# Attention and ELU layer on one core: the probabilities of four groups are turned by VectorE and a round trip through DRAM

## The chip, the core and the metric

One core of a Trainium2 chip runs the whole program. The metric is the device time of one execution in microseconds (us). The kernel before took 598.57 us, the median of 3 runs (598.29 to 599.19). A measurement of this kernel can tell about 0.2% (1.2 us) from no change.

## The reference

Four batches, eight heads, 576 positions, 64 features per head. Each head is causal softmax attention plus a read of a memory matrix; both are mixed by a gate, and the result goes through a two-layer network with ELU. All in float32.

```python
scores = np.where(causal, -1e9, q @ k.T / 8)
a = np.exp(scores - scores.max(-1)); a /= a.sum(-1)
local = a @ v
q_p = phi(q)
mem_out = (q_p @ M_prev) / (q_p @ z_prev)
x = g * mem_out + (1 - g) * local
h = x @ w_in
out = np.where(h > 0, h, np.exp(h) - 1) @ w_out
```

`x` has 2304 rows of 512, `w_in` is 512 x 2048 and `w_out` 2048 x 512.

## The kernel before

The 2304 rows are cut into nine groups of 256. Group 0 holds the first 64 positions of all four batches. Groups 1 to 4 hold positions 64 to 319 of one batch each (`hf` = 0), and groups 5 to 8 hold positions 320 to 575 (`hf` = 1, up to 576 keys). Attention runs by groups in that order, and within a group by four pairs of heads. The network runs in 144 chunks, 16 for each group; a chunk is 128 of the 2048 hidden features. Three groups are split in two parts, so that the network can start while weights still arrive.

Attention of one head in groups 5 to 8, for each of two blocks of 128 queries (`j`):

- scores on TensorE (`add_split`, L787), the product of a key tile with a high and a low part of the query;
- the mask and the row maximum on VectorE (`add_red`, L801), into a row `pt` of 128 queries by 512 or 640 columns, of which the first 64 hold the memory query (`add_mem`, L545);
- the exponential on ScalarE (L832), the reciprocal of the sum on VectorE (L553, L556), and the scaling of the probabilities on ScalarE, VectorE or GpSimd (L848, L850, L852);
- `add_blocks`: each 128 x 128 block of the row is transposed by TensorE against an identity matrix (L878) into a PSUM tile `t`, and copied, nearly always by ScalarE, into `pth` in SBUF (L884). The first block of queries has 4 blocks in one copy, the second has 5 in two copies (3 and 2);
- `pv` in `add_pair` (L739): the turned rows are multiplied with the memory matrix and the values. From group 3 on, one step takes four heads (two pairs) at once, 40 matmuls in groups 5 to 8. It needs the `pth` of all four.

A chunk of the network (`add_ff`) is 12 matmuls of 256 columns (L901), an ELU on ScalarE and VectorE (L916, L919, L922, L931, L934), and 6 matmuls of 512 columns (L965).

The order of all work is made when the program is built. `Plan` holds operations with a priority, the engines that may do each and what each takes by formulas (`dve`, `act`, `dma`, ...), and `Plan.order` plays them through: the operation that can start first goes next, and the priority settles ties. The result is one fixed order of instructions per engine; on the chip an engine waits at an instruction that isn't ready, even if a later one is. All DMAs are issued by SyncE (SP), in that same order. `UBEG`, `UDUE` and `P_ADD` set the priorities of attention by group, `W_ADD` those of the weights. A DMA is taken to land `DMA_LAT` = 2600 ns after its own cost.

A `Ring` is a set of buffers given out in order (`RB` has their numbers). `p` has 2 buffers (one pair of heads), `pth` 4 (two pairs), `kq` 1, `st` 2 (raw weights, and output rows), `wf` 2 (weights in work), `ev` 3 (parts of sums on their way to DRAM).

Of the kernel before, what the change touches and what calls it, by code (L numbers as in the profile page):

```python
# [22 lines left out]
HALF_NK = (320, 576)  # L23
HALF_QCS = ((1, 2), (3, 4))
HALF_NCH = (3, 5)
HALF_RUNS = (((0, 0, 192), (1, 0, 320)),), (((0, 0, 448), (1, 0, 64)), ((1, 64, 576),))
PITCH = 512
SIGN = -0x80000000
REBIAS = 2.0 ** -112
MASKED = -8e9  # L30
# [9 lines left out]
SN = 2  # L40
TN = 2
SPLIT = (4, 7, 11)
UDUE = (-29, 4, 17, 55, 62, 81, 65, 101, 114)
UBEG = (-44, -1, 11, 22, -4, 67, 91, 58, 99)
RB = {'mn': 10, 'rs': 4, 'p': 2, 'pth': 4, 'v': 4, 'ks': 1, 'qh': 1, 'ql': 1, 'kq': 1, 'ev': 3}
BIAS = {'POOL': -400, 'DVE': -150, 'DV2': -250, 'ACT': -750}
E_OFF = 162
FIRST_ACT = 4
# [2 lines left out]
RELU_PHI = 0  # L51
PHI_MIN = -1
W_LATE = (1, 0, -4, -14)
W_ADD = (0, 6, -1, 0, -1, -2, -8, 3, 1, -3, -3, -1, 5, 11, -8, 0, 4, -5, 1, 8, 16, -16, -5, 2, -10, 1, 2, 7, -10, -18, 1, 1)
P_ADD = (-19, -2, 17, 2, -1, 0, -1, 1, 0, -1, 0, 0, 0, -1, -1, -2, -10, 18, -15, -1, 0, 0, 1, -17, 0, -10, 7, -7, 10, -2, 8, 9, 5, 10, 0, -1)
W_OFF = 4
SLACK = 0
WARM_BEG = 1100.0
# [244 lines left out]
def kernel(  # L303
# [22 lines left out]
        kw = {"space": bass.MemoryType.PSUM} if psum else {}  # L326
        return Ring(ctx.enter_context(tc.tile_pool(name=name, bufs=bufs, **kw)), name, bufs, shape, dtype)

    kq_r = ring("kq", RB.get("kq", 2), [128, 832])
    v_r = ring("v", RB.get("v", 2), [128, 6, 64])  # L330
    qz_r = ring("qz", RB.get("qz", 2), [128, 8, 64])
    ks_r = ring("ks", RB.get("ks", 1), [128, S], F32R)
# [4 lines left out]
    p_r = ring("p", RB.get("p", 2), [128, 1152])  # L337
    mn_r = ring("mn", RB.get("mn", 8), [128, 4])
    rs_r = ring("rs", RB.get("rs", 3), [128, 4])
    pth_r = ring("pth", RB.get("pth", 3), [128, 1152])  # L340
    ev_r = ring("ev", RB.get("ev", 2), [128, G])
    xh_r = ring("xh", RB.get("xh", 3), [128, 4, G], F32R)
    xl_r = ring("xl", RB.get("xl", 3), [128, 4, G], F32R)
# [316 lines left out]
    def add_pair(u, pair, qp, rn):  # L660
        b, hf = units[u]
        nk, nch, q0h = HALF_NK[hf], HALF_NCH[hf], HALF_Q0[hf]
        h0 = 2 * pair
        p0 = unit_prio(u, (h0 - 0.5) / NH)
        vs = []
        if hf == 0:
            v = v_r.new()

            def ld_v():
                nc.sync.dma_start(  # L670
                    out=v.t.rearrange("p (h c) d -> p h c d", h=2), in_=vx[b, h0:h0 + 2, :, 0:3].rearrange("h p c d -> p h c d")
                )
# [12 lines left out]

        pts, pths, rs = [p_r.new() for _ in range(2)], [pth_r.new() for _ in range(2)], rs_r.new()
        for i in range(2):
            add_mem(p0, qp, rn, pts[i], 2 * i, 2, PITCH)
        mns = {}
        runs = (HALF_RUNS if NATIVE[u] else RUN_SPLIT)[hf]  # L690
        if NATIVE[u]:
            kqt = kq_r.new()
            if hf == 0:
                add(p0 - 4, [("SP", dma(0.5 * (nk + G)), lambda: nc.sync.dma_start(out=kqt.t[:, 0:nk + G], in_=kqp[b, pair]))], w=[kqt])
            else:
                for i in range(2):
                    def ld(i=i):
                        nc.sync.dma_start(out=kqt.t[64 * i:64 * i + 64, 0:nk + G], in_=kq1[b, h0 + i, 0:64])

                    add(p0 - 4, [("SP", dma(0.25 * (nk + G)), ld)], w=[(kqt, i)])  # L700
            for n, run in enumerate(runs):
                add_scores(u, h0, n / len(runs), run, kqt, nk, pts, mns)
        else:
            for i in range(2):
                kqt = kq_r.new()

                def ld(kqt=kqt, i=i):
                    nc.sync.dma_start(out=kqt.t[:, 0:nk + G], in_=(kq0, kq1)[hf][b, h0 + i])

                add(p0 - 4 + i, [("SP", dma(0.5 * (nk + G)), ld)], w=[kqt])  # L710
                split = split_head(u, h0 + i, kqt)
                for n, run in enumerate(runs):
# [12 lines left out]
        for c in range(nch):
            lo = max(0, (128 * c - 64) - q0h) if c else 0
            mm.append((c, lo, c * G + (0 if c == 4 else lo)))
        late.append([(*vs[i], pths[i]) for i in range(2)])
        if PV_TWO[u] and len(late) < 2:
            return  # L730
        ps = t_r.new()
        todo = late[:]
        late.clear()

        def pv():
            for n, heads in enumerate(todo):
                for i, (c, lo, o) in enumerate(mm):
                    for j, (vj, v0, tj) in enumerate(heads):
                        nc.tensor.matmul(  # L739
                            ps.t[64 * j:64 * j + 64, G * n + lo:G * n + G], vj.t[:, v0 + c], tj.t[:, o:o + G - lo],  # L740
                            start=(i == 0), stop=(i == len(mm) - 1),
                        )

        pp = unit_prio(u, (h0 + 2) / NH)
        cost = TURN_V + len(todo) * sum(pe4(G - lo) for c, lo, o in mm)
        add(pp, [("PE", cost, pv)], r=[x for heads in todo for vj, _, tj in heads for x in (vj, tj)], w=[ps])
        for n in range(len(todo)):
            add_x(u, pp, ps, pair - len(todo) + 1 + n, G * n)
# [3 lines left out]
    def split_head(u, h, kqt):  # L752
# [2 lines left out]
        p0 = unit_prio(u, (h - 0.5) / NH)  # L755
        ks, qh, ql = ks_r.new(), qh_r.new(), ql_r.new()

        def k_hi(eng):
            return lambda: eng(ks.t[:, 0:nk], kqt.t[:, 0:nk])

        def k_lo(eng):
            return lambda: eng.tensor_tensor(
                ks.t[64:128, 0:nk], kqt.t[64:128, 0:nk], ks.t[64:128, 0:nk].bitcast(F32), op=ALU.subtract
            )

        def q_hi(eng):
            return lambda: eng(qh.t, kqt.t[:, nk:nk + G])

        def q_lo(eng):
            return lambda: eng.tensor_tensor(ql.t, kqt.t[:, nk:nk + G], qh.t.bitcast(F32), op=ALU.subtract)  # L770

        add(p0, [("DV2", dve2(nk), k_hi(nc.vector.tensor_copy)), ("ACT", act(nk), k_hi(nc.scalar.copy))], r=[kqt], w=[ks])
        add(p0, [("POOL", pool2(nk), k_lo(nc.gpsimd)), ("DV2", dve(nk), k_lo(nc.vector))], r=[kqt], w=[ks])
# [62 lines left out]
    def add_probs(u, h, j, pt, rs, col, pk, pth):  # L836
# [24 lines left out]
        nblk = qc + 1
        for a, e in ([(0, nblk)] if nblk <= 4 else [(0, 3), (3, nblk)]):
            add_blocks(u, p0, hf, j, a, e, pt, po, pk, pth)

    def add_blocks(u, p0, hf, j, a, e, pt, po, pk, pth):
        ps = t_r.new()
        n = (e - a) * 128
        q0 = 128 * j

        def dst():  # L870
            if a:
                return pth.t[:, a * G + q0:].rearrange("p (c q) -> p c q", q=128)
            m = min(HALF_NCH[hf], 4)
            return pth.t[:, 0:m * G].rearrange("p (c q) -> p c q", q=G)[:, a:e, q0:q0 + 128]

        def tr():
            for c in range(a, e):
                nc.tensor.matmul(  # L878
                    ps.t[:, 128 * (c - a):128 * (c - a) + 128], pt.t[:, po + 128 * c:po + 128 * c + 128], ident,
                    start=True, stop=True, is_transpose=True,  # L880
                )

        def copy(eng):
            return lambda: eng(dst(), ps.t[:, 0:n].rearrange("p (c q) -> p c q", q=128))  # L884

        add(p0, [("PE", 109 * (e - a), tr)], r=pk + [(pt, "m")], w=[ps])
        add(p0, [("ACT", act(n, False), copy(nc.scalar.copy)), ("DVE", dve(n), copy(nc.vector.tensor_copy))], r=[ps], w=[(pth, (j, a))])


    part = nc.dram_tensor('part', (3 * G, DM), F32, kind='Internal').ap()  # L890
    acc_of = {}

    def add_ff(g, c, c0, c1, v):
# [85 lines left out]
        if c1 < NFC:  # L979
# [1 line left out]
                for i in range(2):  # L981
                    add_part(g, t, i, acc[t], pe_)
            return
        osb = st_r.new()

        def view(t):
            return osb.t[:, 512 * t:512 * t + 512].bitcast(F32)

        def fetch(t):
            return lambda: nc.sync.dma_start(out=view(t), in_=part[128 * (2 * g + t):128 * (2 * g + t) + 128])  # L990
# [14 lines left out]

        for t in range(2):
            if c0:
                add(v - 3, [("SP", 800, fetch(t))], r=[f"part{g}{t}"], w=[(osb, t)])
            e_ = "DVE" if c0 or t else "ACT"
            add(pe_, [(e_, (act(512, False) if e_ == "ACT" else dve(512)), ev(t))], r=[acc[t]], w=[(osb, t)])  # L1010
            add(pe_, [("SP", 800, st(t))], r=[(osb, t)])

    def add_part(g, t, i, acc, p):

# [126 lines left out]
```

## Time and profile before

| | before |
|---|---|
| median of 3 runs | 598.57 us (598.29 to 599.19) |
| profiled execution, span from first to last instruction | 597.6 us |
| profiled execution, own time | not listed apart from the span |
| TensorE (PE) busy | 586.7 us, 98% |
| VectorE (DVE) busy | 442.0 us, 74% |
| ScalarE (ACT) busy | 381.1 us, 64% |
| GpSimd (POOL) busy | 73.0 us, 12% |
| DMA moved | 63.85 MB in 32,813 packets |

The span begins with the program's first instruction and ends with its last. Busy time is the time in which at least one instruction of the engine runs. TensorE's matmuls overlap one another, so the sum of their durations exceeds their busy time, and what one costs is read from the distance between starts.

### The profile page before, as it was taken

Reading aid. Unit: us, or ns where it says so; the run is one execution under the profiler, and the core shown is the slowest. Engines: PE = TensorE matmul, PEld = TensorE weight load, DVE = VectorE, ACT = ScalarE, POOL = GpSimd, SP = SyncE. Lnnn points to the kernel's source line nnn. Section 1 sums busy time; section 2 is a strip of 40 time slices with the busy share of each in tenths; the row PEclk is TensorE's granted clock in tenths of the full one; section 3 lists DMA queues with packets and bytes.
Section 4 is the critical chain, followed back from the end, with each engine's and each line's share of the span. In section 5 each row is a group of like instructions: output and inputs, shape, how many; then the busy total and the mean of one; then the engine's idle time right before and its main releaser. Section 6 shows DMA issues by size and latency. Waiting matters only on the chain.

```text
span 597.6 us, 11969 instructions
## 1 busy us (share of the span) xinstructions
PE 586.7 (98%) x4150; PEld 507.0 (85%) x4150; DVE 442.0 (74%) x1394; ACT 381.1 (64%) x1021; POOL 73.0 (12%) x108
## 2 busy tenths in 40 slices
PE   8999999999999999999999999999999999999997
PEld 6766868898898898999888999898889888899996
DVE  6999999999987884477774478687968786444443
ACT  5699889676677872377682377686767776533222
POOL 3333123120011120000120000101111010000000
PEclk9999999999999999999999999999999999999999
DMA  8755756445463332012422022424232323000000
GB/s 264 234 189 183 220 158 209 160 163 185 144 184 113 96 127 72 1 59 90 137 74 59 1 94 74 117 72 154 73 118 74 103 92 103 1 2 28 10 1 36
DMA packets 32813, 63.85 MB, mean 107 GB/s; under 512 B 3568, under 2 KB 17392, under 8 KB 32752
## 3 DMA queue, kind: packets, MB, share of 16 engines
q1 hardware_dynamic: 32752, 63.08, 33.5%
q8 instruction: 33, 0.54, 0.4%
q14 instruction: 28, 0.23, 0.1%
HBM read 56.77 MB, written 6.29 MB: 106 GB/s over the span
## 4 chain that ended last, share of the span: by engine, by line
PE 83%; DVE 12%; ACT 2%; issue 1%; DMA 1%; POOL 0%; DVEq 0%; ACTq 0%; POOLq 0%; SPq 0%
PE acc L965 31%; PE h L901 31%; PE t L739 7%; PE t L878 7%; PE s L787 6%; DVE p L801 2%; DVE st L403 1%; PE acc L1033 1%; DVE wf L406 1%; ACT p L848 1%; DMA p<-in_kqf 1%; DVE gl L934 1%; DVE e L919 1%; DVE p L545 1%; DVE qp L470 1%
## 5 line engine op out<-in xcount | busy, mean ns | idle before, releaser
L901 PE MATMUL h<-xh,w1h 128*128 128x256 f32 x576 | 149.4, 284 | 0.5 <-DVE e L922 0.5
L901 PE MATMUL h<-xl,w1h 128*128 128x256 f32 x576 | 148.1, 281 | 0.0
L901 PEld LDWEIGHTS h<-xh,w1h 128*128 128x128 f32 x576 | 108.4, 188 | 11.9 <-DVE e L922 1.0
L901 PEld LDWEIGHTS h<-xl,w1h 128*128 128x128 f32 x576 | 108.9, 189 | 9.6
L916 ACT ACTIVATE e<-h 128x256 f32<-128x256 f32 x144 | 55.1, 383 | 64.7 <-PE h L901 64.0
L931 ACT CAST gh<-e 128x256 fp32r<-128x256 f32 x143 | 57.8, 404 | 59.2 <-DVE e L922 56.4
L965 PE MATMUL acc<-w2h,gl 128*128 128x512 f32 x288 | 93.5, 403 | 0.0
L965 PE MATMUL acc<-w2h,gh 128*128 128x512 f32 x288 | 92.4, 402 | 0.4 <-ACT gh L931 0.4
L965 PE MATMUL acc<-w2l,gh 128*128 128x512 f32 x288 | 92.8, 402 | 0.0
L901 PEld LDWEIGHTS h<-xh,w1l 128*128 128x128 f32 x576 | 85.0, 189 | 9.2 <-issue 0.5
L901 PE MATMUL h<-xh,w1l 128*128 128x256 f32 x576 | 92.7, 283 | 0.0
L832 ACT ACTIVATE p<-p,mn 128x192 f32<-128x192 f32 (+3 forms) x128 | 78.6, 616 | 18.1 <-DVE mn L801 17.9
L919 DVE TENSOR_SCALAR e<-e 128x256 f32<-128x256 f32 x144 | 43.7, 303 | 51.8 <-ACT e L916 50.4
L934 DVE TENSOR_TENSOR gl<-e,gh 128x256 fp32r<-128x256 f32 x131 | 57.3, 438 | 31.7 <-ACT gh L931 30.9
L884 ACT COPY pth<-t 128x384 f32<-128x384 f32 (+2 forms) x155 | 67.2, 455 | 11.5 <-PE t L878 10.4
L878 PE MATMUL t<-ident,p 128*128 128x128 f32 x448 | 69.3, 274 | 1.2 <-POOL p L852 0.6
L801 DVE CUSTOM_DVE_ANT_0 p<-s,mask 128x192 f32<-128x192 f32 (+3 forms) x128 | 57.9, 476 | 14.8 <-PE s L787 9.7
L878 PEld LDWEIGHTS t<-ident,p 128*128 128x128 f32 x448 | 53.5, 140 | 12.4 <-ACT p L848 2.2
L922 DVE SCALAR_TENSOR_TENSOR e<-h,e 128x256 f32<-128x256 f32 x144 | 60.6, 421 | 2.2
L739 PE MATMUL t<-pth,v 128*64 128x256 f32 (+1 forms) x512 | 54.5, 357 | 1.7 <-ACT pth L884 1.7
L739 PEld LDWEIGHTS t<-pth,v 128*64 128x64 f32 x512 | 34.9, 137 | 20.8 <-ACT pth L884 3.4
L848 ACT ACTIVATE p<-p,rs 128x320 f32<-128x320 f32 (+3 forms) x88 | 47.1, 584 | 6.6 <-DVE rs L556 5.2
(97 smaller groups left out, 818.6 us busy)
## 6 DMA issues: line engine op xcount, KB each, us to landing
kq<-in_kq SPq DMA_DIRECT2D x32, 416.0 KB, 3.1
st<-in_w_in SPq DMA_DIRECT2D x16, 512.0 KB, 3.4
st<-in_w_out SPq DMA_DIRECT2D x16, 512.0 KB, 3.6
qz<-in_qzx SPq DMA_DIRECT2D x32, 224.0 KB, 2.9
v<-in_vx SPq DMA_DIRECT2D x32, 160.0 KB, 2.4
out<-st SPq DMA_DIRECT2D x16, 256.0 KB, 2.1
kq<-in_kqp SPq DMA_DIRECT2D x12, 288.0 KB, 3.3
v<-in_vx SPq DMA_DIRECT2D x16, 192.0 KB, 3.4
```

The costliest lines, as they stand in the source:

```text
L739: nc.tensor.matmul(ps.t[64 * j:64 * j + 64, G * n + lo:G * n + G], vj.t[:, v0 + c], tj.t[:, o:o + G - lo], start=(i == 0), stop=(i == len( ...
L801: nc.vector.tensor_tensor_reduce(out=pts[i].t[:, po + 64 + a:po + 64 + e], in0=ps.t[:, o:o + e - a], in1=m, op0=ALU.add, op1=ALU.min, scal ...
L832: nc.scalar.activation(out=x, in_=x, func=AF.Exp, bias=mn.t[:, 0:1], scale=-1.0, accum_out=rs.t[:, col:col + 1])
L848: eng.activation(out=x, in_=x, func=AF.Copy, scale=c)
L878: nc.tensor.matmul(ps.t[:, 128 * (c - a):128 * (c - a) + 128], pt.t[:, po + 128 * c:po + 128 * c + 128], ident, start=True, stop=True, is_ ...
L884: return lambda: eng(dst(), ps.t[:, 0:n].rearrange("p (c q) -> p c q", q=128))
L901: nc.tensor.matmul(ps.t[:, 0:G], w[:, c, k], x.t[:, k], start=(k == 0 and w is w1h and x is xh), stop=(k == 3 and lo))
L916: nc.scalar.activation(out=at(ee), in_=ps.t[:, 0:G], func=AF.Exp)
L922: nc.vector.scalar_tensor_tensor(at(gg), ps.t[:, 0:G], 0.0, e.t, ALU.max, ALU.add)
L931: return lambda: eng(gh.t, at(gg))
L934: return lambda: eng.tensor_tensor(gl.t, at(gg), gh.t.bitcast(F32), op=ALU.subtract)
L965: nc.tensor.matmul(acc[t].t, a.t[:, 128 * t:128 * t + 128], w[:, c], start=(c == c0 and i == 0), stop=(c == c1 - 1 and i == 2))
```

## The change

In groups 5 to 8 the blocks are no longer transposed by TensorE. For each head and each block of queries VectorE transposes the row in 32 x 32 blocks into `pth`, with the four 32-column strips of the queries side by side (`STEP` = 160 columns each). That leaves the keys spread over the four quadrants of partitions in the wrong order; so each quadrant (32 partitions, 1280 columns) is written to a DRAM buffer `turned` by a DMA of its own, in runs of 160 elements, and one DMA reads the whole 128 x 1280 tile back into the same `pth`. GpSimd clears the columns that the shorter row doesn't fill. `pv` reads its moving operand in runs of 32 elements. Groups 1 to 4 keep the TensorE transposes; the branch for two copies goes away, since at most four blocks are left there.

To make room, `pth` grows to 1280 columns, `kq` shrinks to 576; the keys and queries of groups 5 to 8 are loaded into the `st` ring (2 buffers); output rows go through `wf`; `ev` has 2 buffers. The order constants are new. The branch of `NATIVE` groups with `hf` = 1, which was never taken, is dropped.

```diff
+STEP = 160
-UDUE = (-29, 4, 17, 55, 62, 81, 65, 101, 114)
-UBEG = (-44, -1, 11, 22, -4, 67, 91, 58, 99)
-RB = {'mn': 10, 'rs': 4, 'p': 2, 'pth': 4, 'v': 4, 'ks': 1, 'qh': 1, 'ql': 1, 'kq': 1, 'ev': 3}
+UDUE = (-29, 4, 19, 53, 54, 49, -1, 69, 100)
+UBEG = (-44, -1, 11, 22, 14, 43, 35, 52, 67)
+RB = {'mn': 10, 'rs': 4, 'p': 2, 'pth': 4, 'v': 4, 'ks': 1, 'qh': 1, 'ql': 1, 'kq': 1, 'ev': 2}
...
+def dvt(n):
+    return 145 + 1.1 * n
...
-    kq_r = ring("kq", RB.get("kq", 2), [128, 832])
+    kq_r = ring("kq", RB.get("kq", 2), [128, 576])
-    pth_r = ring("pth", RB.get("pth", 3), [128, 1152])
+    pth_r = ring("pth", RB.get("pth", 3), [128, 8 * STEP])
...
             add_mem(p0, qp, rn, pts[i], 2 * i, 2, PITCH)
+            if hf:
+                add_pad(p0, pths[i])
...
-                kqt = kq_r.new()
+                kqt = (kq_r, st_r)[hf].new()
...
                 add_probs(u, h0 + i, j, pts[i], rs, 2 * i + j, pk[i][j], pths[i])
+            if hf:
+                add_turn(u, h0 + i, pths[i])
...
+                        if hf:
+                            x = tj.t.rearrange("p (s x) -> p s x", x=STEP)[:, lo // 32:8, 32 * c:32 * c + 32]
+                            y = y.rearrange("p (s x) -> p s x", x=32)
...
+        n = (qc + 1) * 128
+        if hf:
+            def turn():
+                x = pt.t[:, po:po + n].rearrange("p (m a i) -> p a m i", a=4, i=32)
+                y = pth.t[:, 4 * STEP * j:4 * STEP * j + 4 * STEP].rearrange("p (a k) -> p a k", k=STEP)[:, :, 0:n // 4]
+                nc.vector.transpose(y.rearrange("p a (m i) -> p a m i", i=32), x)
+
+            add(p0, [("DVE", dvt(n), turn)], r=pk + [(pt, "m")], w=[(pth, j)])
+            return
...
+    def add_pad(p, pth):
+
+        def f():
+            nc.gpsimd.memset(pth.t[:, 0:4 * STEP].rearrange("p (a k) -> p a k", k=STEP)[:, :, 128:STEP], 0.0)
+
+        add(p, [("POOL", 250, f)], w=[(pth, "pad")])
+
+    def add_turn(u, h, pth):
+
+        n = (u - 1 - NB) * NH + h
+        p0 = unit_prio(u, (h + 0.5) / NH)
+        place = turned[128 * n:128 * n + 128]
+
+        def put(c):
+            def f():
+                nc.sync.dma_start(
+                    out=place.rearrange("(a i) (t c x) -> i t a c x", i=32, t=2, c=4)[:, :, :, c],
+                    in_=pth.t[32 * c:32 * c + 32].rearrange("i (t a x) -> i t a x", t=2, a=4),
+                )
+            return f
+
+        for c in range(4):
+            add(p0, [("SP", dma(160), put(c))], r=[pth], w=[(f"turned{n}", c)])
+        add(p0, [("SP", dma(640), lambda: nc.sync.dma_start(out=pth.t, in_=place))], r=[f"turned{n}"], w=[pth])
+
+    turned = nc.dram_tensor('turned', (NB * NH * 128, 8 * STEP), F32, kind='Internal').ap()
...
-        osb = st_r.new()
+        osb = [wf_r.new() for t in range(2)]
```

`W_ADD` and `P_ADD` are new number by number; those of `W_ADD` now go from -58 to 25 (before from -18 to 16), those of `P_ADD` for groups 5 to 8 from -35 to 46 (before from -17 to 10).

## Rows read from the trace of the kernel before

**Rows 1.** The page: busy time by engine, and 40 slices for PE and its clock.

```profile
PE 586.7 (98%) x4150; PEld 507.0 (85%) x4150; DVE 442.0 (74%) x1394; ACT 381.1 (64%) x1021; POOL 73.0 (12%) x108
PE   8999999999999999999999999999999999999997
PEclk9999999999999999999999999999999999999999
```

**Rows 2.** Busy time by stretch: PE, PEld, DVE, ACT, POOL, clock, DMA share, GB/s.

```profile
0.00:30.00 30.00, 26.92 (x299) 21.36 (x300) 23.47 (x110) 18.35 (x66) 9.53 (x18) 1.00 0.77 249
30.00:90.00 60.00, 56.96 (x389) 41.83 (x387) 59.17 (x197) 53.14 (x162) 15.62 (x24) 1.00 0.59 189
205.00:523.00 318.00, 317.70 (x2244) 280.50 (x2240) 225.70 (x705) 203.19 (x511) 28.88 (x43) 1.00 0.26 82
523.00:597.60 74.60, 70.62 (x451) 63.13 (x446) 30.71 (x79) 21.61 (x54) 0.00 (x0) 0.99 0.04 15
```

**Rows 3.** Waits of PE: us in total, times, longest.

```profile
PE acc L1033 <- POOL ident masks.py:199: 1.8, 1, 1.8
PE t L739 <- ACT pth L884: 1.7, 3, 0.8
```

**Rows 4.** Groups by line: the transposes; then the copies L884 alone, by stretch (DVE, ACT).

```profile
L878 PE MATMUL t<-ident,p 128*128 128x128 f32 x448 | 69.3, 274 | 1.2 <-POOL p L852 0.6 <-ACT p L848 0.5
...
205.00:523.00 318.00, 2.88 (x5) 44.57 (x99) 1.00 0.26 82
```

**Rows 5.** Timeline of PE around seven transposes: start, length of the merged run, instruction.

```profile
485.67 0.62 PE L965 MATMUL acc<-w2h,gl 128*128 128x512 f32 x2
486.13 0.28 PE L901 MATMUL h<-xh,w1h 128*128 128x256 f32 x1
...
486.60 0.93 PE L878 MATMUL t<-ident,p 128*128 128x128 f32 x7
487.29 0.71 PE L965 MATMUL acc<-w2h,gh 128*128 128x512 f32 x2
487.83 0.40 PE L965 MATMUL acc<-w2l,gh 128*128 128x512 f32 x1
```

**Rows 6.** Groups by line on DVE, shapes apart: busy us, mean ns.

```profile
L850 DVE TENSOR_SCALAR p<-p,rs 128x576 f32<-128x576 f32 x15 | 8.1, 548 | 0.1
L762 DVE TENSOR_TENSOR ks<-kq,ks 64x576 fp32r<-64x576 f32 x32 | 25.0, 781 | 1.6 <-ACT ks L759 0.7
L997 DVE COPY st<-acc 128x512 f32<-128x512 f32 x6 | 4.1, 689 | 1.5 <-PE acc L965 1.5
```

**Rows 7.** DMA: the queue's packets, MB, share; issues with KB and us to landing.

```profile
q1 hardware_dynamic: 32752, 63.08, 33.5%
...
st<-in_w_out SPq DMA_DIRECT2D x16, 512.0 KB, 3.6
...
v<-in_vx SPq DMA_DIRECT2D x32, 160.0 KB, 2.4
...
part<-ev SPq DMA_DIRECT2D x12, 128.0 KB, 2.5
```

**Rows 8.** Instructions of L681 and L1022 on SP: issue ns min/median/max, first and last start.

```profile
L681 SPq DMA_DIRECT2D v<-in_vx x32: 327/382/431, 205.4 to 496.7; - x32
...
L1022 SPq DMA_DIRECT2D part<-ev x12: 319/354/1473, 62.8 to 136.8; - x12
```

**Rows 9.** Timeline of PE at the last product with the values.

```profile
519.11 4.11 PE L739 MATMUL t<-pth,v 128*64 128x256 f32 x40
523.15 0.62 PE L901 MATMUL h<-xh,w1l 128*128 128x256 f32 x3
```

**Rows 10.** Waits of the DMA queue, the longest of the key loads.

```profile
SPq L708 <- DVE ql L770: 69.0, 14, 25.4
```

**Rows 11.** Groups by line on POOL: the memset of 128 columns.

```profile
masks.py:197 POOL MEMSET ident<- 128x128 f32 x1 | 0.2, 205 | 0.3 <-POOLq L1131 0.3
```

More of the change, by code (lines that the diff above doesn't have):

```diff
@@ L25 @@
 HALF_NCH = (3, 5)
-HALF_RUNS = (((0, 0, 192), (1, 0, 320)),), (((0, 0, 448), (1, 0, 64)), ((1, 64, 576),))
+HALF_RUNS = ((0, 0, 192), (1, 0, 320)),
 PITCH = 512
+STEP = 160
 SIGN = -0x80000000
@@ L53 @@
 W_LATE = (1, 0, -4, -14)
-W_ADD = (0, 6, -1, 0, -1, -2, -8, 3, 1, -3, -3, -1, 5, 11, -8, 0, 4, -5, 1, 8, 16, -16, -5, 2, -10, 1, 2, 7, -10, -18, 1, 1)
-P_ADD = (-19, -2, 17, 2, -1, 0, -1, 1, 0, -1, 0, 0, 0, -1, -1, -2, -10, 18, -15, -1, 0, 0, 1, -17, 0, -10, 7, -7, 10, -2, 8, 9, 5, 10, 0, -1)
+W_ADD = (16, -20, -1, 0, -1, 6, -8, 5, 19, -5, -3, 1, 7, -19, -8, 10, 6, 5, 1, -26, 20, -16, -19, 4, -22, -7, 2, -47, -8, -58, 25, -19)
+P_ADD = (-19, -2, 17, 2, -3, 0, -1, 1, -4, -1, -4, 0, 6, 1, -1, -2, -18, 26, -41, -5, -20, -30, 1, -13, -10, 20, -21, -7, 46, 0, 16, 5, 19, 2, -8, -35)
 W_OFF = 4
@@ L688, in add_pair @@
             add_mem(p0, qp, rn, pts[i], 2 * i, 2, PITCH)
+            if hf:
+                add_pad(p0, pths[i])
         mns = {}
-        runs = (HALF_RUNS if NATIVE[u] else RUN_SPLIT)[hf]
+        runs = HALF_RUNS if NATIVE[u] else RUN_SPLIT[hf]
         if NATIVE[u]:
             kqt = kq_r.new()
[L693 to L700, printed above, removed]
+            add(p0 - 4, [("SP", dma(0.5 * (nk + G)), lambda: nc.sync.dma_start(out=kqt.t[:, 0:nk + G], in_=kqp[b, pair]))], w=[kqt])
             for n, run in enumerate(runs):
@@ L704, in add_pair @@
             for i in range(2):
-                kqt = kq_r.new()
+                kqt = (kq_r, st_r)[hf].new()
                 def ld(kqt=kqt, i=i):
-                    nc.sync.dma_start(out=kqt.t[:, 0:nk + G], in_=(kq0, kq1)[hf][b, h0 + i])
+                    nc.sync.dma_start(out=kqt.t.bitcast(F32)[:, 0:nk + G], in_=(kq0, kq1)[hf][b, h0 + i])
                 add(p0 - 4 + i, [("SP", dma(0.5 * (nk + G)), ld)], w=[kqt])
@@ L738, in pv @@
                     for j, (vj, v0, tj) in enumerate(heads):
[L739 to L742, printed above, removed]
+                        x, y = tj.t[:, o:o + G - lo], ps.t[64 * j:64 * j + 64, G * n + lo:G * n + G]
+                        if hf:
+                            x = tj.t.rearrange("p (s x) -> p s x", x=STEP)[:, lo // 32:8, 32 * c:32 * c + 32]
+                            y = y.rearrange("p (s x) -> p s x", x=32)
+                        nc.tensor.matmul(y, vj.t[:, v0 + c], x, start=(i == 0), stop=(i == len(mm) - 1))
         pp = unit_prio(u, (h0 + 2) / NH)
@@ L756, in split_head, with kq @@
         ks, qh, ql = ks_r.new(), qh_r.new(), ql_r.new()
+        def kq():
+            return kqt.t.bitcast(F32)
         def k_hi(eng):
-            return lambda: eng(ks.t[:, 0:nk], kqt.t[:, 0:nk])
+            return lambda: eng(ks.t[:, 0:nk], kq()[:, 0:nk])
         def k_lo(eng):
             return lambda: eng.tensor_tensor(
-                ks.t[64:128, 0:nk], kqt.t[64:128, 0:nk], ks.t[64:128, 0:nk].bitcast(F32), op=ALU.subtract
+                ks.t[64:128, 0:nk], kq()[64:128, 0:nk], ks.t[64:128, 0:nk].bitcast(F32), op=ALU.subtract
             )
         def q_hi(eng):
-            return lambda: eng(qh.t, kqt.t[:, nk:nk + G])
+            return lambda: eng(qh.t, kq()[:, nk:nk + G])
         def q_lo(eng):
-            return lambda: eng.tensor_tensor(ql.t, kqt.t[:, nk:nk + G], qh.t.bitcast(F32), op=ALU.subtract)
+            return lambda: eng.tensor_tensor(ql.t, kq()[:, nk:nk + G], qh.t.bitcast(F32), op=ALU.subtract)
         add(p0, [("DV2", dve2(nk), k_hi(nc.vector.tensor_copy)), ("ACT", act(nk), k_hi(nc.scalar.copy))], r=[kqt], w=[ks])
@@ L859, in add_probs @@
         ], r=[(rs, col)], w=pk)
[L861 to L865, printed above, removed]
+        n = (qc + 1) * 128
[6 more added lines that the diff above has]
+            return
         ps = t_r.new()
-        n = (e - a) * 128
         q0 = 128 * j
[L870 to L874, printed above, removed]
         def tr():
-            for c in range(a, e):
+            for c in range(qc + 1):
                 nc.tensor.matmul(
-                    ps.t[:, 128 * (c - a):128 * (c - a) + 128], pt.t[:, po + 128 * c:po + 128 * c + 128], ident,
+                    ps.t[:, 128 * c:128 * c + 128], pt.t[:, po + 128 * c:po + 128 * c + 128], ident,
                     start=True, stop=True, is_transpose=True,
@@ L883, in copy, with f @@
         def copy(eng):
-            return lambda: eng(dst(), ps.t[:, 0:n].rearrange("p (c q) -> p c q", q=128))
-        add(p0, [("PE", 109 * (e - a), tr)], r=pk + [(pt, "m")], w=[ps])
-        add(p0, [("ACT", act(n, False), copy(nc.scalar.copy)), ("DVE", dve(n), copy(nc.vector.tensor_copy))], r=[ps], w=[(pth, (j, a))])
+            def f():
+                o = pth.t[:, 0:HALF_NCH[0] * G].rearrange("p (c q) -> p c q", q=G)[:, 0:qc + 1, q0:q0 + 128]
+                eng(o, ps.t[:, 0:n].rearrange("p (c q) -> p c q", q=128))
+            return f
+        add(p0, [("PE", 109 * (qc + 1), tr)], r=pk + [(pt, "m")], w=[ps])
+        add(p0, [("ACT", act(n, False), copy(nc.scalar.copy)), ("DVE", dve(n), copy(nc.vector.tensor_copy))], r=[ps], w=[(pth, j)])
+    def add_pad(p, pth):
[7 more added lines that the diff above has]
+        def put(c):
+            def f():
+                nc.sync.dma_start(
+                    out=place.rearrange("(a i) (t c x) -> i t a c x", i=32, t=2, c=4)[:, :, :, c],
+                    in_=pth.t[32 * c:32 * c + 32].rearrange("i (t a x) -> i t a x", t=2, a=4),
+                )
+            return f
+        for c in range(4):
+            add(p0, [("SP", dma(160), put(c))], r=[pth], w=[(f"turned{n}", c)])
+        add(p0, [("SP", dma(640), lambda: nc.sync.dma_start(out=pth.t, in_=place))], r=[f"turned{n}"], w=[pth])
+    turned = nc.dram_tensor('turned', (NB * NH * 128, 8 * STEP), F32, kind='Internal').ap()
     part = nc.dram_tensor('part', (3 * G, DM), F32, kind='Internal').ap()
@@ L983, in add_ff @@
             return
-        osb = st_r.new()
+        osb = [wf_r.new() for t in range(2)]
         def view(t):
-            return osb.t[:, 512 * t:512 * t + 512].bitcast(F32)
+            return osb[t].t.bitcast(F32)
         def fetch(t):
@@ L1007, in add_ff @@
             if c0:
-                add(v - 3, [("SP", 800, fetch(t))], r=[f"part{g}{t}"], w=[(osb, t)])
+                add(v - 3, [("SP", 800, fetch(t))], r=[f"part{g}{t}"], w=[osb[t]])
             e_ = "DVE" if c0 or t else "ACT"
-            add(pe_, [(e_, (act(512, False) if e_ == "ACT" else dve(512)), ev(t))], r=[acc[t]], w=[(osb, t)])
-            add(pe_, [("SP", 800, st(t))], r=[(osb, t)])
+            add(pe_, [(e_, (act(512, False) if e_ == "ACT" else dve(512)), ev(t))], r=[acc[t]], w=[osb[t]])
+            add(pe_, [("SP", 800, st(t))], r=[osb[t]])
     def add_part(g, t, i, acc, p):
```

## The prediction

> **What bounds the kernel now.** I read the busy times first, then the stretches, then the waits of PE. PE is busy for 586.7 of 597.6 us, and its granted clock is that of the higher level (2.4 GHz) in all 40 slices [rows 1]. By stretches, PE lacks 3.1 us in the first 30 us and 3.0 us in the next 60; from 205 to 523 us, where attention of groups 5 to 8 runs between chunks of the network, it lacks 0.3 us of 318 [rows 2]. Its longest sums of waiting are 1.8 us, once at the start, and 1.7 us in three waits for a copied `pth` [rows 3]. So the end is set by the amount of work on PE: what leaves PE leaves the time, unless a new wait takes its place. No other engine is near that: from 205 to 523 us DVE is busy for 225.7 us, ACT for 203.2, POOL for 28.9, and the DMA engines have a share of 0.26 [rows 2].
>
> The profiled span is 597.6 us. The page lists no own time beside it; the median is 0.97 us above it, and I carry that over unchanged.
>
> **Removed: 288 transposes on PE.** Groups 5 to 8 have 4 x 8 heads with 4 + 5 blocks: 288 of the 448 [rows 4]. What does one cost? Seven start at 486.60, and the next matmul starts at 487.29: 0.69 us. But then two L965 take 0.54 us until the next start, where two took 0.46 us at 485.67 [rows 5]; those 0.08 us belong to the transposes. 0.77 / 7 = 0.110 us, and the sum is 288 x 0.110 = **31.7 us**. The mean of 274 ns [rows 4] is the duration of an instruction that overlaps its neighbours and is not this cost; the group's busy 69.3 / 448 = 155 ns isn't either, since it counts the tail that lies over the next matmul.
>
> The Trainium skill (TensorE: Matmul & The Clock Gate, Part 4: PE-mode transpose) gives about 275 ns for a transpose in one kernel. The trace agrees with that as a duration. As a cost it would make 288 x 0.275 = 79 us, against the distances above.
>
> **Removed: 96 copies.** ACT loses nearly all of the 44.6 us of L884 between 205 and 523 us, DVE at most 2.9 us [rows 4]. ACT isn't the bound: 0 from the time, but room for ACT to take work from DVE.
>
> **Added: 64 transposes on DVE**, 32 of 512 and 32 of 640 columns. No row shows one. The nearest: 0.689 us for a copy of 512 columns, 0.781 for a two-operand step of 576, 0.548 for a one-operand step of 576 in which both halves go side by side [rows 6]. At 548 ns per 576 columns, 64 x 0.548 = 35 us; at 0.689 us per 512, scaled to the mean of 576 columns, 64 x 0.775 = 49.6 us; at twice that, if 32-bit elements go through at half rate, 99 us. I take 49.6, the plain copy. DVE from 205 to 523 us would have 225.7 - 2.9 + 49.6 = 272 of 318 us, and 46 idle: 0 from the time. It costs if that cover goes (rival 2).
>
> **Added: the round trip.** Each head writes 128 x 1280 x 4 bytes = 655 KB in 4 DMAs of 1024 packets of 640 bytes in all, and reads 655 KB back in 128 rows; 32 heads make 41.9 MB.
>
> - SP issues 5 x 32 = 160 more DMAs, 0.354 to 0.382 us each [rows 8], 57 to 61 us spread over some 300. Behind a readback that waits for its writes stand the loads of keys, values and queries and the stores of the output. The keys get a second buffer (`st`), while the single one made SP wait 69 us for DVE [rows 10], so they can be in SBUF before they are needed: 0.
> - DMA engines: 33.5% of 597.6 us is 200 us for 63.08 MB [rows 7], 3.17 us per MB. At that price the 41.9 MB take 133 us beside the 0.26 x 318 = 83 us that are there: 216 of 318 us. If instead each 640-byte packet took what the mean packet of 1926 bytes took (200 x 16 / 32752 = 98 ns), the writes would take 32768 x 98 / 16 = 201 us instead of 66, and the sum would be 351 of 318. I take the price per byte, since it is the same in stretches with unlike mixes of rows, 0.77 / 249 in the first 30 us and 0.26 / 82 later, 3.1 and 3.2 us per MB [rows 2]: 0 from the time, with the other end kept as rival 3.
> - Delay of one head: 4 issues (1.5 us), the last write lands after 2.4 to 2.5 us, and the readback in about 4.0 us (2.4 us at 160 KB, 3.6 at 512 KB, drawn on to 640) [rows 7, 8]: 8.0 us. The built order counts 4 x 0.496 + 2.6 + 1.984 + 2.6 = 9.2 us, so PE finds `pth` there at the 8 steps of `pv`, with 1.2 us to spare. I allow 0.4 us a step, half of the longest wait that a `pth` has caused [rows 3]: **+3 us**, between 0 and 6.
>
> **The rest.** The memset on POOL, 32 x 0.205 us = 6.6 us [rows 11], fits in POOL's 289 idle us: 0. It waits for the `pv` before, and POOL's memory queries and scalings queue behind it; they belong to the same pair, which has to wait for the same buffer. `pv` itself, 8 x 4.04 us [rows 9], now reads runs of 32 elements at a pitch of 160. No row has such an operand on PE: 0 if only the count of columns matters, up to 32 us if it goes at half rate; I take 0, since the count stays. `ev` with 2 buffers makes the sums of three groups leave PSUM a store later, 0 to 3 x 2.5 us [rows 7]; other chunks' first products can run meanwhile: 0. New order constants up to 205 us: PE lacks 6.1 us there in the first 90 us [rows 2], so a better order gives at most 6, a worse one may cost as much: 0.
>
> Sum: 598.57 - 31.7 + 3 = **570 us**.
>
> **Is attention early enough?** After the last `pv` (523.15 us) 451 matmuls run [rows 2, 9], 25 chunks of 18; the last group needs 16. So 9 chunks, some 25 us, lie between, and a turn of 8 us, even with the stretch 31 us shorter, leaves some room if attention starts where it does now (205 us [rows 8]) and runs with fewer pauses.
>
> **Rivals.**
>
> 1. *The moving operand in runs of 32 slows `pv`.* For: no row excludes it. Against: PE takes one column after another from each partition, in equal numbers. At half rate 8 x 4.04 = 32 us come back: 599; midway 583. Chance 0.05.
> 2. *DVE becomes the bound between 205 us and the last `pv`.* For: 272 of 318 us are close, and the stretch must shrink: PE ends near 567, the last 16 chunks need 45 (18 x 70.62 / 451 = 2.82 us each [rows 2]), so attention must be done by about 518. DVE then has 313 - 272 = 41 us. It decides when a transposition takes more than 0.775 + 41/64 = 1.4 us. At 1.55 us the lack is 99 - 91 = 8 us, and with lags of the ELU on DVE twice that: 575 to 585. Against: ACT is relieved of 45 us and may take casts and scalings. Chance 0.12.
> 3. *Slower: the round trip comes later than the fixed order assumes.* Place: the 8 steps of `pv`. PE stands there with chunks queued behind it; DVE's next transpose waits for the same four `pth` buffers, with the ELU steps L919, L922 and L934 queued behind. Price: whatever the trip takes over 9.2 us, times 8; it decides at 31.7 / 8 = 4.0 us a step, a trip of 13.2 us. At 98 ns a packet a head's writes take 6.3 instead of 2.1 us and the trip 12.2 us: 8 x 3.0 = 24 us, and the DMA engines lack 351 - 318 = 33 us besides, of which the 25 us of room cover most: 567 + 24 + 10 = 601, and 590 to 620 around it. Against: the landing times above. Chance 0.17. The Trainium skill (DMA: Bandwidth & Descriptors, Rules for kernel authors) goes further: to turn data by a plain DMA with a rearranged access pattern is 19 times slower than the hardware's own DMA transpose. Here a run is 640 bytes and not one element. If the writes did go at a nineteenth of the price per byte, 66 x 19 = 1254 us of DMA would set the time, over 1400 us; I give that 0.01 of the 0.17.
> 4. *A transpose costs PE its whole 274 ns.* Then 79 us go: 598.57 - 78.9 + 3 = 523. Against: seven of them start within 0.69 us [rows 5]. Chance 0.01. It is the price that the page on TensorE, named above as the Trainium skill's, would give.
>
> The forecast has the rest, 0.65: 564 to 577, by waits from 0 to 6 us and the early part from -3 to +4.
>
> **Range and chances.** The range holds the forecast (0.65), nearly all of rival 2, the half of rival 1 that lies midway, and the nearer edge of rival 3: 562 to 595. Faster by over 0.2% (1.2 us, what a measurement can tell from no change): 0.65 + 0.12 + 0.01 + 0.03 of rival 1 and 0.01 of rival 3 = 0.82. Same: 0.03, where rivals 1 and 3 pass by 598. Slower: 0.15, the rest of rival 3 and a little of 1.
>
> **What would show it.** Right: L878 x160 instead of x448; PE still near 98% of a span near 569 us; DVE near 490 us busy with 64 transposes near 0.7 and 0.85 us; the waits of PE at L739 on the readback under 6 us in all; `turned` writes landing within 3 us and readbacks within 4.5; DMA share between 205 and 520 us near 0.7. Wrong: PE idle in front of L739 by over 3 us a step (rival 3), distances over 0.2 us between the pairs of matmuls in `pv` (rival 1), DVE without pauses from 205 us on and PE waiting for DVE at L965 or L787 (rival 2).

## The result, and the profile after

| | before | after |
|---|---|---|
| median | 598.71 us (598.29 to 599.19, 4 runs) | 568.18 us (567.52 to 569.10, 4 runs) |
| span of the profiled execution | 597.6 us | 566.7 us |
| its own time | not listed | 568.52 us |

The ratio is 0.9491 (95% interval 0.9477 to 0.9506): 30.5 us less (29.6 to 31.3). The forecast was 570 us.

First the page of the kernel after, parts 1 and 2, and its DMA queue (part 3).

```profile
PE 555.5 (98%) x3857; PEld 478.4 (84%) x3857; DVE 461.7 (81%) x1404; ACT 343.8 (61%) x933; POOL 109.6 (19%) x186
...
PEclk9999999999999999999999999999999999999999
...
q1 hardware_dynamic: 72176, 105.03, 59.2%
```

Then busy time by stretch, with the columns of [rows 2].

```profile
30.00:90.00 60.00, 57.85 (x397) 43.88 (x396) 59.35 (x196) 52.99 (x162) 18.06 (x25) 1.00 0.61 196
90.00:205.00 115.00, 114.03 (x768) 100.05 (x767) 101.95 (x296) 78.11 (x213) 21.70 (x31) 1.00 0.48 153
205.00:500.00 295.00, 294.88 (x2000) 258.99 (x1999) 249.76 (x737) 174.30 (x447) 61.29 (x113) 1.00 0.72 221
500.00:566.70 66.70, 62.72 (x410) 55.05 (x408) 26.96 (x69) 18.09 (x46) 0.74 (x1) 1.00 0.18 56
```

PE is 98% busy as before [rows 1], with 31.2 us less busy time, and lacks 0.1 us of the 295 in which the attention of groups 5 to 8 runs. In that stretch DVE rose from 71% [rows 2] to 85% and the DMA share from 0.26 to 0.72. The waits of PE answer to [rows 3] (us in total, times, longest):

```profile
PE acc L1065 <- POOL ident masks.py:199: 1.8, 1, 1.8
PE t L641 <- DVE rn L498: 1.2, 1, 1.2
PE t L881 <- ACT p L854: 0.7, 2, 0.5
```

No wait for the readback is among them, nor among the smaller ones. The transposes that are left on PE answer to [rows 4], those of DVE to [rows 6] (groups by line, shapes apart):

```profile
L881 PE MATMUL t<-ident,p 128*128 128x128 f32 x160 | 26.7, 276 | 1.2 <-ACT p L854 0.7 <-issue 0.3 <-ACT pth L889 0.2
...
L872 DVE STREAM_TRANSPOSE pth<-p 128x640 f32<-128x640 f32 x32 | 26.1, 824 | 3.9 <-PE t L745 3.8
L872 DVE STREAM_TRANSPOSE pth<-p 128x512 f32<-128x512 f32 x32 | 22.1, 690 | 3.5 <-PE t L745 3.5
```

The new DMAs on SP answer to [rows 8] (issue ns min/median/max) and, with their landing times, to [rows 7]:

```profile
L910 SPq DMA_DIRECT2D turned<-pth x128: 569/617/1747, 242.3 to 504.5; - x128
...
DMA to landing us min/median/max: 2.5/2.7/4.7
...
L918 SPq DMA_DIRECT2D pth<-turned x32: 319/462/1559, 247.8 to 508.8; - x32
...
DMA to landing us min/median/max: 3.9/4.7/7.0
```

Four issues of 0.617, a landing of 2.7 and one of 4.7 us make 9.9 us. With the waits in between, a trip takes 10.8 us, from the end of a head's second transpose on DVE to the landing of its readback (median of the 32 heads, worked out from the trace's times).

The last product with the values answers to [rows 9] (timeline of PE):

```profile
511.28 4.11 PE L745 MATMUL t<-pth,v 128*64 128x256 f32 x40
515.32 0.50 PE L997 MATMUL acc<-w2h,gh 128*128 128x512 f32 x1
```

And all instructions of that line, after and then before (duration ns min/median/max, first and last start; the counts by shape at the end are of every third instruction):

```profile
L745 PE MATMUL t<-pth,v x512: 272/379/431, 33.2 to 515.1; 128*64 128x256 f32 x137, 128*64 128x128 f32 x34
...
L739 PE MATMUL t<-pth,v x512: 272/379/431, 34.7 to 523.0; 128*64 128x256 f32 x137, 128*64 128x128 f32 x34
```

A product takes 4.04 us to the next start, as before: runs of 32 elements cost PE nothing. The last one's last matmul starts at 515.1 us, 51.6 us before the end; before it was 74.7 us (522.95 to 597.62). The last product is followed by 298 matmuls; the last group's 16 chunks are 288 of them, so that 51.6 us are little more than these chunks and the store. So the reserve of some 9 chunks is used up.

### The profile page after: what moved, and what is told of

Read it like the earlier page. It is cut to its first block, busy times and chain, and to the rows that moved or that the text cites. A ratio compares the mean times of both kernels' runs of the same rounds, so it can differ in the third digit from the quotient of the medians.

```text
span 566.7 us, 11765 instructions
## 1 busy us (share of the span) xinstructions
PE 555.5 (98%) x3857; PEld 478.4 (84%) x3857; DVE 461.7 (81%) x1404; ACT 343.8 (61%) x933; POOL 109.6 (19%) x186
## 3 DMA queue, kind: packets, MB, share of 16 engines
q1 hardware_dynamic: 72176, 105.03, 59.2%
## 4 chain that ended last, share of the span: by engine, by line
PE 85%; DVE 9%; ACT 2%; DMA 2%; issue 1%; SPq 0%; ACTq 0%; DVEq 0%
PE acc L997 33%; PE h L933 33%; PE t L745 8%; PE s L793 6%; PE t L881 2%; DVE p L807 2%; PE acc L1065 1%; ACT p L854 1%; PE s L825 1%; DVE st L408 1%; DVE e L951 1%; DVE wf L411 1%; DMA igate<-in_beta 1%; DVE e L954 1%; DMA p<-in_kqf 1%
## 5 line engine op out<-in xcount | busy, mean ns | idle before, releaser
L838 ACT ACTIVATE p<-p,mn 128x320 f32<-128x320 f32 (+3 forms) x128 | 78.4, 614 | 24.2 <-DVE mn L807 23.3
L951 DVE TENSOR_SCALAR e<-e 128x256 f32<-128x256 f32 x144 | 45.4, 315 | 36.7 <-ACT e L948 35.9
L966 DVE TENSOR_TENSOR gl<-e,gh 128x256 fp32r<-128x256 f32 x119 | 52.6, 442 | 17.0 <-ACT gh L963 15.5
L745 PE MATMUL t<-pth,v 128*64 128x256 f32 (+1 forms) x512 | 54.1, 356 | 0.5 <-ACT pth L889 0.5
L872 DVE STREAM_TRANSPOSE pth<-p 128x512 f32<-128x512 f32 (+1 forms) x64 | 47.1, 757 | 7.4 <-PE t L745 7.3
L745 PEld LDWEIGHTS t<-pth,v 128*64 128x64 f32 x512 | 35.4, 137 | 19.1 <-ACT pth L889 1.8
L854 ACT ACTIVATE p<-p,rs 128x192 f32<-128x192 f32 (+3 forms) x85 | 45.5, 580 | 7.2 <-DVE rs L561 6.0
L997 PEld LDWEIGHTS acc<-w2h,gl 128*128 128x128 f32 x288 | 45.9, 189 | 2.8 <-issue 0.8
L997 PEld LDWEIGHTS acc<-w2l,gh 128*128 128x128 f32 x288 | 45.8, 189 | 2.3 <-issue 1.2
```

The costliest lines, as they stand in the source:

```text
L745: nc.tensor.matmul(y, vj.t[:, v0 + c], x, start=(i == 0), stop=(i == len(mm) - 1))
L838: nc.scalar.activation(out=x, in_=x, func=AF.Exp, bias=mn.t[:, 0:1], scale=-1.0, accum_out=rs.t[:, col:col + 1])
L854: eng.activation(out=x, in_=x, func=AF.Copy, scale=c)
L872: nc.vector.transpose(y.rearrange("p a (m i) -> p a m i", i=32), x)
L951: nc.vector.tensor_scalar(e.t, at(ee), 1.0, -1.0, ALU.min, ALU.add)
L966: return lambda: eng.tensor_tensor(gl.t, at(gg), gh.t.bitcast(F32), op=ALU.subtract)
```

## Experiments

Each starts from the kernel after, if nothing else is said. The costs that `Plan` counts stay as they are, so the order of the instructions is that of the kernel after, and only the named work is added or left out. In the runs with other order constants, and in those with group 4, the order is played through anew.

**288 transposes put back on PE.**

```diff
         def pv():
+            for _ in range(36 if hf else 0):
+                nc.tensor.matmul(ps.t[:, 0:128], ident, ident, start=True, stop=True, is_transpose=True)
```

> The changed kernel in its own order, with 36 transposes of the identity ahead of each of the 8 products of groups 5 to 8, 288 in all, into PSUM columns that the product then overwrites. Theory (a transpose costs TensorE 0.110 us and nothing covers it): 568.2 + 31.7 = 599.9 us, 597 to 602. Rival (what was gained came from the new order or from the relief of ScalarE, and TensorE has room now): under 594 us. A transpose at its whole duration of 274 ns would give 647 us.

Measured: 600.57 us (599.17 to 601.68), 32.4 us more than after; ratio to before 1.0037 (1.0024 to 1.0050). The added group by line:

```profile
L739 PE MATMUL t<-ident 128*128 128x128 f32 x288 | 32.7, 273 | 0.0
```

Here 36 run in a row, so that the busy time is nearly free of overlap with others: 32.7 / 288 = 0.114 us, at a duration of 273 ns each. The price of the removed work is confirmed, and that nothing covered it. ScalarE's copies are not put back, so the gain isn't its relief. The price from durations (79 us) is out.

**The round trip left out.** The writes and the readback are not issued; the last products then run on quadrants that are not exchanged.

```diff
         def put(c):
             def f():
+                return
...
-        add(p0, [("SP", dma(640), lambda: nc.sync.dma_start(out=pth.t, in_=place))], r=[f"turned{n}"], w=[pth])
+        add(p0, [("SP", dma(640), lambda: None)], r=[f"turned{n}"], w=[pth])
```

> The changed kernel in its own order, with the 128 writes to DRAM and the 32 readbacks left out, so that the last products run on probabilities whose quadrants are not exchanged. Theory (TensorE's amount of work sets the end and the round trip is wholly hidden): 567 to 569 us, as the changed kernel's 568.2. Rival (the trip still costs waits that lie under the overlapping ends of matmuls, the 3 us that the forecast allowed): 565.5 us or less.

Measured: 567.65 us (567.56 to 569.13). That is 0.5 us under the kernel after, inside the spread of both. 42 MB through DRAM and 160 DMAs cost nothing that these runs can tell in this order.

**The trip made longer.** Once by writing every quadrant twice, once by writing only the fourth twice (`[0:2 if c == 3 else 1]` behind the pair of targets), the second time to a buffer that nobody reads.

```diff
-                nc.sync.dma_start(
-                    out=place.rearrange(...
+                for to in (place, spare[128 * n:128 * n + 128]):
+                    nc.sync.dma_start(
+                        out=to.rearrange(...
```

> The changed kernel in its own order, with each quadrant written twice, the second time to a DRAM buffer that nobody reads. DMA engines' share between 205 and 500 us rises from 0.72 to near 0.99 (32768 more packets of 39 ns on 16 engines are 80 us). Theory (the last readback lands 0.5 to 1.9 us before the second half of each of the 8 products needs it, and a trip that is some 3 us longer eats that): 576 to 586 us, with TensorE idle inside or ahead of the products. Rival (the order has more room than that): under 571 us. Third (the DMA engines run full and a backlog grows): over 595 us.

Measured: 638.67 us (636.99 to 643.65), ratio to before 1.0686 (1.0640 to 1.0732): 70.5 us more than after, well past what the theory allowed. With all four written twice, the longest wait of PE:

```profile
PE t L745 <- DMA pth<-turned: 43.7, 12, 7.7
```

The page's 40 slices for PE and its clock:

```profile
PE   8999999999999999979969699799598895996997
...
PEclk9999999999999999979979989899699798897999
```

And the stretch that holds the eight products:

```profile
240.00:570.00 330.00, 290.25 (x1808) 246.83 (x1807) 224.15 (x648) 150.69 (x379) 56.98 (x103) 0.92 0.85 248
```

The DMA engines are not full: 0.85, not 0.99. The trip is longer, 17.9 us against 10.8 (the same median): 4.9 instead of 1.9 us between the first and the last issue, 2.7 instead of 0.8 us until the first, while SP is still at other DMAs, and 1.0 us in slower landings (medians, which do not add up to the whole). The readback waits for the second writes too (SP does so 20 times, 17.7 us in all). PE idles up to 7.7 us at a product, and its granted clock has a mean of 0.92 in the stretch: the slices below 9 in the clock's row are ones with an idle PE in them or just ahead. The trace has the lower level (1.2 GHz) eight times, once at each product, during its wait or right behind it, for 6.8 or 10.2 us, 58 us in all. One of them:

```profile
322.00:328.80 6.80, 5.51 (x23) 3.46 (x24) 0.00 (x0) 0.65 (x2) 0.78 (x3) 0.50 0.12 35
```

The eight products, from their first start to the start of the next matmul, take 97.1 us here and 8 x 4.04 = 32.3 in the kernel after: 64.7 of the 69.2 us that the span is longer. Waiting is 43.7 us of it by the row above. In the eight stretches at the lower level PE is busy for 39.8 us, which cost at most half of that, 20 us. So 70.5 / 8 = 8.8 us a product for 7.1 us of trip are some 5.5 us of waiting and up to 2.5 us of lower clock behind it.

> The changed kernel in its own order, with the fourth quadrant of each head written a second time, to a DRAM buffer that nobody reads: one more DMA of 0.62 us of issue per head, where writing all four twice made the trip 7.1 us longer and the kernel 70 us. Theory A (each of the 8 products has some room, the 0.5 to 1.9 us by which the last readback lands before the second half needs it): 568 to 572 us. Theory B (every us of trip costs a us at every product; the trip grows by 0.8 to 1.5 us): 574 to 582 us.

Measured: 572.62 us (569.52 to 575.27), 4.4 us more than after, between the two theories. The trip is 12.7 us, 1.9 more; the eight products lose 0.55 us each. They take 37.0 us in all by the distances between starts (4.0 to 5.5 each) instead of 32.3, so the loss is in them. If each us of trip past the room costs a us, a product has 1.3 us of room. In the trace of the kernel after, the last readback landed 0.5 to 1.9 us before the second half of its product began, 1.4 in the mean. PE's waits for the readback, of which this view sees only a part, since it counts idle time behind the modelled end of a matmul:

```profile
PE t L745 <- DMA pth<-turned: 1.3, 3, 0.8
```

**More work on DVE.** Every transpose twice, then only those of the first block of queries (`range(1 if j else 2)`).

```diff
-                nc.vector.transpose(y.rearrange("p a (m i) -> p a m i", i=32), x)
+                for _ in range(2):
+                    nc.vector.transpose(y.rearrange("p a (m i) -> p a m i", i=32), x)
```

> The changed kernel in its own order, with each of the 64 transposes on VectorE done twice: 47.1 us more of VectorE's work, where it was idle for 45 of the 295 us between 205 and 500. Theory (VectorE has hardly any room left there, and in a fixed order what it does late reaches TensorE): 578 to 600 us. Rival (the idle time can be used, because the chunks of the network run ahead): under 573 us.

> The changed kernel in its own order, with the transposes of the first block of queries alone done twice: 22.1 us more of VectorE's work, where twice all of them (47.1 us) cost 39.6 us. Theory A (VectorE has no idle time that a fixed order can use; in proportion): 18.6 us, 583 to 590 us. Theory B (the first 7 to 10 us are free, and then each us counts): 579 to 583 us. Rival (most of it is absorbed): under 575 us.

Measured: 607.77 us (605.97 to 609.15) and 583.95 us (581.99 to 584.73), that is 39.6 us more for 47.1 us of DVE work, 7.8 us past the top of what was expected, and 15.8 for 22.1, which is in theory A's range. The slope between the two is 23.8 / 25.0 = 0.95; on a straight line, some 22.1 - 15.8 / 0.95 = 5 us would be free and the rest count nearly in full. That is an upper end. With all transposes doubled the clock was at the lower level three times for 3.4 us, which the run with half of them has not; that costs at most 5.1 us, and without it the slope is 0.75 and only some 1 us would be free. So theory B's 7 to 10 free us are not there. With all transposes doubled, the longest waits of PE:

```profile
PE h L934 <- DVE e L955: 18.6, 13, 2.9
PE s L793 <- DVE mn L807: 6.5, 8, 2.1
```

And two stretches:

```profile
205.00:350.00 145.00, 133.84 (x875) 115.61 (x874) 128.94 (x359) 77.76 (x206) 24.24 (x44) 0.98 0.60 181
350.00:500.00 150.00, 138.25 (x901) 118.93 (x900) 134.26 (x355) 77.31 (x197) 32.14 (x58) 0.98 0.72 218
...
307.60:311.00 3.40, 3.40 (x13) 3.06 (x12) 3.09 (x12) 2.02 (x5) 0.74 (x1) 0.50 0.82 178
```

DVE is 89% busy there, not 100%, and PE waits for it at the ELU and at the row maxima. Each of the eight products takes 4.04 us, so the trip is not what comes late. The last line is the first of the three stretches at the lower clock.

**The order and the change taken apart.** First the kernel after with the old `UDUE`, `UBEG`, `P_ADD`, `W_ADD`; then the kernel before with the new ones.

```diff
-UDUE = (-29, 4, 19, 53, 54, 49, -1, 69, 100)
-UBEG = (-44, -1, 11, 22, 14, 43, 35, 52, 67)
+UDUE = (-29, 4, 17, 55, 62, 81, 65, 101, 114)
+UBEG = (-44, -1, 11, 22, -4, 67, 91, 58, 99)
...
```

> The changed kernel with the four lists of order constants of before (due and start times of attention, their additions, additions of the weights). Theory (TensorE's work is the bound and almost any order that keeps it fed gives the gain): 568 to 576 us. Rival (the round trip and VectorE's longer work fit only in the new order): over 582 us.

> The kernel before with the new order constants alone, its transposes on TensorE. Theory (the constants serve the new work and save TensorE nothing): 598 to 606 us. Rival (part of the 30.5 us is the better order): under 597 us.

Measured: 605.51 us (604.46 to 607.62), ratio to before 1.0118 (1.0098 to 1.0138), and 604.52 us (603.73 to 605.97), ratio 1.0100 (1.0083 to 1.0116). Neither half is a gain: the new work in the old order is 7 us slower than before, the new order without it 6 us slower, both together 30.5 us faster. In the old order, the instructions of L745:

```profile
L745 PE MATMUL t<-pth,v x512: 272/379/689, 34.4 to 551.4; 128*64 128x256 f32 x137, 128*64 128x128 f32 x34
```

And the stretch in which it falls behind:

```profile
350.00:500.00 150.00, 134.58 (x845) 113.25 (x844) 123.34 (x367) 81.13 (x202) 25.08 (x48) 0.93 0.79 242
```

The last product's last matmul starts at 551.4 us, 36.3 us later than in the kernel after, and the span (602.6 us) is 35.9 us longer. Both DVE and the trip are late there: between 350 and 500 us PE waits 6.1 us for row maxima and 3.7 for keys from DVE, and three of the eight products take 5.7 to 10.1 us. How the 36 us divide between them isn't shown. The new order without the change has its last product early, with the last start at 509.4 us, but PE lacks 4.4 us between 90 and 205 us, before any of the changed groups (0.5 us in the kernel before):

```profile
90.00:205.00 115.00, 110.64 (x745) 96.31 (x743) 101.14 (x295) 74.49 (x204) 11.46 (x20) 1.00 0.45 144
```

**Group 4 turned as well**, 40 transposes fewer on PE; then with order constants made for it.

```diff
+TURNED = (0, 0, 0, 0, 1, 1, 1, 1, 1)
...
-            if hf:
+            if TURNED[u]:
                 add_turn(u, h0 + i, pths[i])
...
```

> The changed kernel with group 4 turned in the same way: 40 more transposes leave TensorE, VectorE gets 16 more (256 and 384 columns, some 0.45 us each, 7 us), and 8 more round trips, some 10 MB. The order constants stay. Theory (TensorE's work is the bound, so 40 x 0.110 = 4.4 us go): 563.5 to 566 us. Rival (VectorE is busy for 102 of 115 us between 90 and 205 us, where most of group 4's attention runs, and the order wasn't made for it): 568 to 575 us.

> Group 4 turned as well, now with order constants made anew for that (four lists, found by playing the order through many times with changed numbers and keeping those that end earlier). Theory (what stands in the way of the 40 transposes' 4.4 us is when attention ends, and that is the order's to set): 563 to 566 us, with the last product with the values near 511 us. Rival (between 205 and 500 us the DMA engines and VectorE are too full for 8 more round trips, whatever the order): 567 to 574 us.

Measured: 573.68 us (573.14 to 575.85), ratio to before 0.9593 (0.9574 to 0.9611), and 568.83 us (568.18 to 570.16), ratio 0.9497 (0.9484 to 0.9510): slower than the kernel after, then level with it. In the first, the last product begins 0.7 us later than in the kernel after and takes 8.2 us instead of 4.0, which is most of the 4.7 us that the span is longer: its readback is late, and 6.8 us at the lower clock follow. The wait:

```profile
PE t L746 <- DMA pth<-turned: 2.0, 1, 2.0
```

With its own order, two stretches:

```profile
90.00:205.00 115.00, 111.81 (x743) 96.76 (x744) 104.70 (x306) 74.57 (x208) 22.42 (x36) 1.00 0.59 186
205.00:350.00 145.00, 143.11 (x962) 124.49 (x961) 121.73 (x359) 83.51 (x217) 40.45 (x73) 1.00 0.82 252
```

PE lacks 3.2 and 1.9 us here, against 1.0 and none in the same stretches after: the 4.4 us of work that left PE come back as 4 us of waiting. DVE has to do group 4's transposes where it is 91% busy, but that it is what PE waits for isn't shown: between 90 and 350 us PE's longest wait is 1.7 us, for ACT, and its waits for DVE come to 1.1 us. Whether a better order exists stays open.

**Where each ends.** In ten of these kernels the last matmul of the last product starts 51 to 53 us before the end:

| kernel | last matmul of `pv` starts | span |
|---|---|---|
| before | 523.0 us | 597.6 us |
| new order alone | 509.4 us | 601.9 us |
| after | 515.1 us | 566.7 us |
| trip left out | 514.3 us | 565.9 us |
| PE transposes back | 548.2 us | 599.8 us |
| writes twice | 583.2 us | 635.9 us |
| fourth write twice | 519.4 us | 571.0 us |
| DVE transposes twice | 554.3 us | 605.9 us |
| DVE transposes of the first block twice | 530.4 us | 582.0 us |
| old order | 551.4 us | 602.6 us |
| group 4 too | 519.3 us | 571.4 us |
| group 4, own order | 516.5 us | 568.1 us |

In the first two, work for PE is piled up behind attention (75 and 93 us), so that the amount of PE's work should count alone; no run delays attention in them to show it. In the others the end of attention sets the end, and whatever delays it (PE, DVE or the trip) is paid in full: 33.1, 39.2 and 68.1 us later there are 33.1, 39.2 and 69.2 us more of span.

## Why the prediction was right

- *What bounds the kernel.* Right. PE stayed at 98%, and putting 288 transposes back cost 32.4 us.
- *The transposes, 31.7 us.* Right: 30.5 us measured in all, and 0.114 us each in the run that put them back. The price that the Trainium skill gives (TensorE: Matmul & The Clock Gate, Part 4: PE-mode transpose), about 275 ns, is again the duration, 273 to 276 ns, and not the cost.
- *The transposes on DVE, 49.6 us hidden.* Right in size (26.1 + 22.1 = 48.2 us) and hidden. But the cover was misjudged: of the 41 us of idle time counted in rival 2 only some 1 to 5 could be used for more work. With 48.2 + 22.1 us, 1.1 us a transpose, the kernel is already 15.8 us slower; I had set the point at 1.4.
- *The round trip, +3 us.* The term that was mis-sized: it is 0 within the spread (567.65 against 568.18 us). Its parts were wrong both ways, and that they cancel is luck. The trip takes 10.8 us and not 8.0: an issue is 0.617 us and not 0.35 to 0.38, the readback lands in 4.7 us and not 4.0 (over the 4.5 that was named as a sign), and SP is busy at the start. By rival 3's own price, 8 times what the trip takes over 9.2 us, that would have cost 13 us. Yet PE doesn't wait: a product begins with the pair of heads that came first and reaches the other pair 2 us later, which the prediction didn't count. At the last one the last readback landed at 512.8 us by the trace, 1.5 us after the product's start.
- *Rival 3, the slower side.* It didn't happen, and its place was right: PE idles at the eight products as soon as the trip is longer. I had set the point at a trip of 13.2 us; the runs have 572.6 us at 12.7 and 638.7 at 17.9, and a straight line between them passes 598.7 at 14.8. Full DMA engines, which I named as the cause, were not what made it late; SP's issues, and the wait for them, were most of it. The Trainium skill's factor of 19 for a turn by plain DMA (DMA: Bandwidth & Descriptors, Rules for kernel authors) isn't tested, since it is against the hardware's own transpose, which no run uses. The slow writes that the prediction drew from it didn't come: 160 KB written in runs of 640 bytes landed in 2.7 us, where 128 KB in rows of 1 KB took 2.5 [rows 7]. (Its "nineteenth of the price" is to be read as 19 times the price, as in its product 66 x 19.)
- *Rival 1.* No: 4.04 us a product before and after.
- *DMA share near 0.7, DVE near 490 us.* The share was 0.72, and the price per byte held: 59.2% of 566.7 us for 105.03 MB is 3.19 us per MB, against 3.17. DVE was busy for 461.7 us, as the order gave more of its work to POOL (busy for 109.6 us instead of 73.0, with 6.6 us of it the new memset) and some to ACT (381.1 to 343.8 us, less of a fall than the 44.6 us of copies).
- *"New order constants: 0".* This looked only at the first 205 us and missed what they are for. The forecast gain was there only with the new order: with the old one the same work takes 605.5 us. The condition stood in the prediction, that attention be done by about 518 us (515.3 measured), but not that the old constants would miss it by 34 us (552.1). The "some room" that it saw there is gone: 10 matmuls beyond the last 16 chunks are left.

## What to carry to other kernels

Work taken off a saturated engine is worth the distance between its instructions' starts, not their durations or busy time; and here it was paid out only with an order made anew for the work that replaces it. Look not only at the bound but at the reserve behind the last dependent stage: here 75 us before the end became 52, the length of the last group, and from there on the latency of that stage, past a room of some 1.4 us a product, costs as much as PE's work or more. Idle time of an engine in a fixed order is no cover by its sum: 45 us idle on DVE hid 1 to 5 us of added work.

## What the runs showed of the hardware

The first was not expected; the other two had been assumed in the prediction, without a row that showed them.

- A DMA whose target is cut in 256 runs of 640 bytes took 0.617 us to issue on SP, against 0.354 and 0.382 us for one of 128 rows [rows 8] and 0.462 for the readback, 128 rows too.
- VectorE's transpose of 32-bit elements goes at the pace of a copy out of PSUM: 690 ns for 128 x 512 and 824 ns for 128 x 640, beside 689 ns for such a copy of 128 x 512 [rows 6]. A one-operand step within SBUF was faster, 548 ns for 128 x 576 [rows 6].
- PE's moving operand in runs of 32 elements at a pitch of 160 costs nothing against a dense one: 4.04 us for 40 matmuls in both kernels.
